# A fused long-convolution and gated-MLP gradient kernel: the order of VectorE's steps in each convolution group, from the product with xn on

## The chip, the cores and the metric

The kernel runs on one core of a Trainium2 chip. The metric is the device time of one execution in microseconds (us), as the median of several. The core has five engines with an instruction stream each: TensorE (PE in the profile, with its weight loads as PEld), VectorE (DVE), ScalarE (ACT), GpSimd (POOL) and SyncE (SP, which here only issues DMA transfers). Matmul results land in PSUM, of which the kernel uses eight banks of 128 x 512 f32; everything else that the engines touch lies in SBUF, and large arrays lie in HBM.

## The reference

The program takes the forward inputs and the gradient of the output, and returns the output and nine gradients, all in bfloat16. S = 2048 rows, D = 1024 channels, F = 3584:

```
x  = A_q
xn = layernorm(x)                                   # over the channels
k_shift[t] = sum_i  k[t - 3 + i] * taps[i]          # 4 taps per channel ("shift")
kv = k_shift * A_v
y  = irfft(rfft(kv, 4096) * rfft(ssm_k, 4096))[:2048] + kv * ssm_D
h  = relu(xn @ W_gate) * (xn @ W_up)
out = x + xn * y + h @ W_down
grads = vjp(out)(grad_out)     # for q, k, v, shift_k, ssm_k, ssm_D, W_gate, W_up, W_down
```

So there are two parts that only share xn. The convolution branch works per channel along time: for the backward pass it needs the gradient of y, which is `grad_out * xn` (the product with xn), its transform, products of spectra for the gradients of kv and of the filter, and then the taps' gradients. The MLP is a chain of large matmuls.

## The kernel before, in words

**MLP.** Class LnMlp. TensorE is fed by it in phases: `hidden` (per 128 rows and 512 of F: gate, up and the gradient of h, eight matmuls of 128x512 each, tiles ps_g, ps_u, ps_h, line L1038), `grad_down` (gradient of W_down, tile ps_d), `grad_in` (gradients of W_gate and W_up, tile ps_w; both L1373, 16 matmuls to a bank), `out_phase` (h @ W_down, tile ps_o, L1537) and `grad_x` (ps_x, L1669). At the ends of `grad_down` and at the start of `grad_in`, where four PSUM banks are accumulated side by side (`four`, L1381 to L1418, matmuls at L1389), the branch may use only two banks at a time instead of three (`self.branch.cap = 2`). In `hidden` VectorE masks up by gate (L1153, tile ru<-ru,ps_u), multiplies (L1159, ht) and, when ScalarE has copied ps_h to gh (L1281), multiplies ru by gh (L1282); the result is stored to ug_d by SP. At the start of `grad_down` grad_out's rows are loaded anew (g_nat, issued by SP at L1068).

**Convolution branch.** Class ABranch. The channels are worked in eight groups of 128, one after the other. The Fourier transforms are small matmuls (all by `mm`, L83) with tables R, FW, IA and RB; ScalarE evicts their results from PSUM (`act`, L87), and VectorE does the products of spectra and the taps (`tt`, L91) and transposes (`flip`, L334: two instructions of 128x1024 f32 for one flip). One large SBUF tile, `arena`, holds all spectra, so most of the branch's rows in the profile read `arena<-arena`.

The blocks on TensorE of one group, in order: `f2` (eight units, three banks' worth at a time; 48, 48 and 32 matmuls with FW), `inv_a` of the gradient, joined with the next group's filter transform (IA and hn,R), `inv_b` for gkv (16 matmuls with RB), `inv[1]` (32 with IA), `cross[0]` and `cross[1]` (half an inverse each, joined with the next group's transform of the product with xn, tile gt), `inv[2]` (32 IA), two `f2` units of the next filter `f2H` (64 FW), again `cross[0]`, `cross[1]` (joined with the next group's kv, tile kp), and then two blocks of 32 FW and 16 RB: `inv_b` for yt (the convolution's output, which goes to y_d) and `inv_b` for gh (the filter's gradient, stored to gh_d).

**How the two are woven.** `slots` (L677) is a generator: each `yield p, d` is one slot, with p the branch's TensorE work (or None) and d its VectorE work: a generator of which one step is taken, a function to be called, or None. `steps` (L577) runs the slots of one group after the other and gives back a nominal time, 1900 ns in `hidden`; in the later phases (`dense`) 1900 for a slot with TensorE work and 1250 for one without. The main loop (after L1764) takes that against what the MLP's generators yield (mostly 1730 ns for eight matmuls): whenever the MLP has caught up, one more slot is emitted. While the branch runs, `pri.strict` pins every instruction, so each engine works in the order in which the program emits it, the MLP's and the branch's together. A VectorE or SP instruction that must wait holds up all that is behind it on its engine. `need` and `fetch` place the loads of the next groups on SP in the same order; a `store` is also emitted at its place.

The VectorE work that the slots name:

- `gate_grad(nx)`: grad_out times xn of the next group, in place, tile gt. With it the part that is changed begins.
- `q`: `cmul`, a product of two half spectra in five steps; here the last, `cmul(H, K, ..., 1)`.
- `tk`: `taps` forward for the next group: four products and three sums, one to a step, seven steps; then `start_kvt`, the product with v.
- `tg`: `taps` backward (tile gk<-gks and gk<-gk,tap), seven steps of 128x2048 bf16.
- `fly`, `flh`, `flG`, `flK`: flips, two steps each; fly is wanted by the yt block, flh by the gh block, flG and flK by the next group's `f2`.

**At the branch's end** `a.close()` frees its SBUF, and `open_right` (L1492) opens the pools of `hT` and `wd` there: W_down is loaded in four pieces of 28 x 128 rows in all (L1498, issued by SP), and `out_phase` loads h transposed (L1503). `out_phase` begins with the first matmul of wd and hT.

Of the kernel before, what the change touches and what calls it, by code (L numbers as in the profile page):

```python
# [48 lines left out]
class ABranch:  # L49
# [627 lines left out]
    def slots(self, st, gi):  # L677
        G, K, H, GKV = self.G, self.K, self.H, self.GKV
        if gi == 0:
            yield from self.first(st)  # L680
        nx, n2 = self.ahead(st, 1), self.ahead(st, 2)
        last = nx is None
        f2 = [(1, self.f2_pair(j, m)) for j in range(4) for m in range(2)]
        if self.cap == 3:
            yield f2[0:3], None
            yield None, None
            yield None, None
            yield f2[3:6], None
        else:
            for i in (0, 2):  # L690
                yield f2[i:i + 2], None
                yield None, None
            yield f2[4:6], None
        yield None, None
        yield None, lambda: self.turn(G, 0, -1, slice(0, 4))
        q = self.cmul(H, G, True, GKV, 0)
        yield f2[6:8], q
        yield None, q
        yield None, q
        yield None, q  # L700
        yield None, q
        yield None, lambda: self.turn(G, 0, -1, slice(4, 8))
        iaG = self.inv_a()
        q = self.cmul(H, G, True, GKV, 1)
        yield None, q
        if last:
            iaG = [iaG[1][0], None, iaG[1][1]]
        else:
            self.need(self.load_filter, nx)
            self.need(self.load_rest, nx)  # L710
            iaG = self.crossed(iaG[0], self.fwd1_filter(nx)[0], 0) + iaG[1][1:]
        yield iaG[0], q
        yield None, q
        yield None, q
        yield iaG[1], q
        yield None, lambda: self.turn(H, 1, 1)
        self.fetch(nx, self.load_k, self.load_taps)
        q = self.cmul(K, G, True, G, 0)
        yield None, q
        yield iaG[2], q  # L720
        yield None, q
        flg = self.flip_C(self.Cg, 0)
        yield None, flg
        yield None, flg
        if not last:
            self.need(self.load_g, nx)
            flH = self.flip_H()
            yield None, self.both(lambda: self.add_D(nx), flH)
            yield None, flH
        yield None, q  # L730
        yield None, q
        q = self.cmul(H, K, False, K, 0)
        yield self.inv_b(st, "gkv", 0), q
        yield None, q
        yield None, q
        gkv = st["gkv"]
        gks = st["gks"] = self.ttile("gks")
        yield None, lambda: self.tt(gks[:, 0:16, :], gkv[:, 0:16, :], st["vt"][:], ALU.mult)
        self.fetch(nx, self.load_v)
        gv = self.ttile("gv")  # L740
        yield None, lambda: self.tt(gv[:, 0:16, :], gkv[:, 0:16, :], st["ksh"][:], ALU.mult)
        yield None, q
        self.store(self.gks_d[gi], gks[:, 0:16, :].rearrange("p r c -> p (r c)"))
        yield None, q
        self.store_time(self.out_gv, st["cg"], gv)
        yield [], lambda: self.halo(st)
        ia, inv = self.inv_a_pair()
        q = self.cmul(K, G, True, G, 1)
        yield inv[1], q
        for _ in range(4):  # L750
            yield None, q
        q = self.cmul(H, K, False, K, 1)
        cross, gk = [inv[0], None], None
        if not last:
            self.need(self.load_xn, nx)
            yield None, lambda: self.gate_grad(nx)
            self.fetch(n2, self.load_xn)
            cross = self.crossed(ia, self.fwd1(self.Bg, nx["gt"])[0], 0)
        yield None, q
        yield None, None  # L760
        yield cross[0], q
        yield None, q
        yield None, q
        yield cross[1], None
        self.fetch(n2, self.load_g)
        yield None, q
        if last:
            f2H, cross = [], [inv[3], None]
            yield inv[2], None
        else:  # L770
            f2H = [(1, self.f2(H, 1, j)) for j in range(4)]
            self.need(self.load_k, nx)
            self.need(self.load_taps, nx)
            self.begin(nx)
            tk = nx["tk"]
            yield None, tk
            yield inv[2], tk
            yield None, tk
            yield None, tk
            yield f2H[0:2], tk  # L780
            yield None, tk
            yield None, tk
            self.need(self.load_v, nx)
            yield None, lambda: self.start_kvt(nx)
            cross = self.crossed(ia, self.fwd1(self.Bk, nx["kvt"])[0], 3)
            yield None, None
        gk = self.ttile("gk")
        tg = self.taps(st, gk, gks, [(0, 0), (1, 1), (2, 2), (3, 3)])
        yield cross[0], tg
        yield None, tg  # L790
        yield None, None
        yield cross[1], tg
        self.fetch(n2, self.load_filter)
        yield None, tg
        yield None, tg
        fly = self.flip_C(self.Cy, 0)
        yield None, fly
        yield None, fly
        yield None, tg
        yield f2H[2:3] + self.inv_b(st, "yt", 0), None  # L800
        self.store_time(self.y_d, st["cg"], st["yt"])
        flh = self.flip_C(self.Ch, 0)
        yield None, flh
        yield None, flh
        yield None, tg
        self.store_time(self.out_gk, st["cg"], gk)
        yield f2H[3:4] + self.inv_b(st, "gh", 0), None
        if last:
            yield None, None
            yield None, lambda: self.store_gh(st)  # L810
            return
        flG = self.flip_B(self.Bg, 0)
        yield None, flG
        yield None, self.both(lambda: self.store_gh(st), flG)
        flK = self.flip_B(self.Bk, 1)
        yield None, flK
        yield None, flK
        yield None, None

A_START = 60_000  # L820
# [996 lines left out]
```

## Time and profile before

| what | value |
|---|---|
| median of 3 runs | 1864.61 us (1864.56 to 1864.93) |
| the profiled execution | 1865.49 us |
| its span, first to last instruction | 1863.7 us |
| TensorE's granted clock | 1.00 |
| busy: PE, DVE, ACT, POOL | 1836.8, 1112.2, 646.7, 19.3 us |

| stretch (us) | phase | PE busy | DVE busy | ACT busy | DMA share |
|---|---|---|---|---|---|
| 60 to 635 | hidden | 567.42 of 575 | 444.22 | 276.93 | 0.78 |
| 635 to 855 | grad_down | 215.12 of 220 | 161.19 | 105.83 | 0.66 |
| 855 to 1280 | grad_in | 419.94 of 425 | 243.72 | 189.66 | 0.59 |
| 1280 to 1467 | out_phase | 186.10 of 187 | 41.15 | 0.59 | 1.10 |
| 1467 to 1863 | grad_x | 391.58 of 396 | 184.25 | 41.96 | 0.74 |

Times in the lines below are us from the span's start, unless a column says otherwise. In a timeline line the first number is the start, the second the duration, then engine, line of the code, operation, tiles (out<-in), shapes and how many instructions the line holds; in square brackets stands how long the engine had been idle before it and who ended that. A line of waits reads: engine, tile and line that waited, who was waited for, then the total in us, how often, and the longest. In a line of windows: stretch, its length, then busy time and count for PE, PEld, DVE, ACT and POOL, the granted clock, the DMA share and GB/s. "xN" in a timeline line is a run of N like instructions. A few matmul records are missing from the trace; such a hole is about 0.22 us wide, one matmul.

### The profile page before, as it was taken

What the parts mean: (1) busy time and instruction counts of PE and PEld (TensorE: products, weight loads), DVE (VectorE), ACT (ScalarE), POOL (GpSimd) and SP (SyncE); (2) the same over time, 40 slices, a digit from 0 to 9 for tenths busy, and PEclk for the clock granted to TensorE, in tenths of its full rate; (3) what the DMA queues carried; (4) which work ended last, traced back from release to release, by engine and by line L of the source; (5) the groups of instructions that cost most, each with busy time, mean ns of one, the idle gap of its engine ahead of it and who ended that gap; (6) DMA issues with size and microseconds to landing.
All of it is one profiled execution on the core that took longest, in us unless ns stands there. A gap on an engine that the chain in (4) does not pass through costs nothing.

```text
span 1863.7 us, 31858 instructions
## 1 busy us (share of the span) xinstructions
PE 1836.8 (99%) x12842; PEld 846.2 (45%) x13061; DVE 1112.2 (60%) x1635; ACT 646.7 (35%) x1215; POOL 19.3 (1%) x51
## 2 busy tenths in 40 slices
PE   9999999999999999999999999999999999999999
PEld 4444444444444444444444444444444544444444
DVE  6656887797788767585594866810212222466652
ACT  5644444535444454545545455320000000111100
POOL 1000000000000000000000000000000000000000
PEclk9999999999999999999999999999999999999999
DMA  9897679968758657558656544479999857799973
GB/s 259 251 220 187 150 200 205 223 163 190 180 150 221 217 147 184 128 163 210 181 146 164 125 133 128 136 176 284 264 240 243 194 135 168 180 209 203 202 163 74
DMA packets 748132, 344.65 MB, mean 185 GB/s; under 512 B 576088, under 2 KB 715344, under 8 KB 747984
## 3 DMA queue, kind: packets, MB, share of 16 engines
q1 hardware_dynamic: 736848, 320.31, 71.4%
q10 hardware_dynamic: 9504, 17.04, 2.9%
q0 software_dynamic: 1632, 5.24, 0.8%
q8 instruction: 102, 1.67, 0.4%
q14 instruction: 46, 0.38, 0.1%
HBM read 143.79 MB, written 103.83 MB: 133 GB/s over the span
## 4 chain that ended last, share of the span: by engine, by line
PE 72%; issue 1%; DVE 0%; DMA 0%; ACT 0%
PE ps_x L1669 21%; PE ps_w L1373 20%; PE ps_o L1537 10%; PE ps_d L1373 9%; PE ps_c L83 3%; PE ps_u L1038 3%; PE ps_h L1038 3%; PE ps_g L1038 2%; PE ps_d L1389 1%; PE ps_w L1389 1%; DVE arena L334 0%; PE ps_r L1571 0%; DMA g_nat<-in_grad_out_dram 0%; ACT arena L87 0%; ACT wi L1413 0%
## 5 line engine op out<-in xcount | busy, mean ns | idle before, releaser
L1373 PE MATMUL ps_w<-ugs,xn_nat 128*128 128x512 bf16 x1674 | 375.8, 379 | 4.4 <-issue 2.4
L87 ACT CAST arena<-ps_c 128x512 bf16<-128x512 f32 x576 | 293.9, 610 | 103.5 <-PE ps_c L83 103.3
L1038 PEld LDWEIGHTS <-xnT 128*128 128x128 bf16 x1792 | 171.4, 98 | 209.4 <-issue 6.4
L334 DVE STREAM_TRANSPOSE arena<-arena 128x1024 f32<-128x1024 f32 x96 | 179.6, 1930 | 134.7 <-ACT arena L87 114.2
L1373 PEld LDWEIGHTS <-xn_nat 128*128 128x128 bf16 x1728 | 165.1, 98 | 201.6 <-issue 7.3
L1038 PE MATMUL ps_u<-wu,xnT 128*128 128x512 bf16 x879 | 205.4, 379 | 0.9
L1038 PE MATMUL ps_g<-wg,xnT 128*128 128x512 bf16 x865 | 202.5, 379 | 1.9 <-DVE xnT L1082 0.3
L1038 PE MATMUL ps_h<-wdT,goT 128*128 128x512 bf16 x864 | 202.3, 379 | 1.8
L1669 PE MATMUL ps_x<-wuT,guT 128*128 128x512 bf16 x878 | 197.5, 379 | 1.0
L1669 PE MATMUL ps_x<-wgT,ggT 128*128 128x512 bf16 x878 | 197.3, 379 | 0.9
L1687 ACT ACTIVATE w<-xn,m 128x512 f32<-128x512 bf16 x32 | 24.3, 807 | 479.5 <-DVE m L1680 366.1
L1537 PE MATMUL ps_o<-wd,hT 128*128 128x512 bf16 (+1 forms) x879 | 186.7, 372 | 0.9
L1373 PE MATMUL ps_d<-g_nat,hs 128*128 128x512 bf16 x742 | 167.2, 379 | 2.2 <-issue 1.3
L1669 PEld LDWEIGHTS <-guT 128*128 128x128 bf16 x896 | 87.7, 98 | 105.7
L1669 PEld LDWEIGHTS <-ggT 128*128 128x128 bf16 x896 | 87.7, 98 | 105.5
L1038 PEld LDWEIGHTS <-goT 128*128 128x128 bf16 x896 | 86.4, 98 | 104.0 <-issue 1.4
L1537 PEld LDWEIGHTS <-hT 128*128 128x128 bf16 x896 | 87.7, 98 | 99.9
L1376 ACT CAST wi<-ps_w 128x512 bf16<-128x512 f32 x108 | 64.4, 596 | 192.3 <-PE ps_w L1373 168.8
L1281 ACT CAST gh<-ps_h 128x512 bf16<-128x512 f32 x112 | 65.9, 591 | 178.7 <-PE ps_h L1038 158.1
L1153 DVE SCALAR_TENSOR_TENSOR ru<-ru,ps_u 128x512 bf16<-128x512 bf16 x112 | 76.4, 682 | 85.5 <-PE ps_u L1038 44.1
L1529 DVE TENSOR_TENSOR ya<-ya,xe 128x1024 bf16<-128x1024 bf16 x16 | 11.1, 692 | 182.6 <-DMA xe<-xn_d 182.6
L91 DVE TENSOR_TENSOR t<-arena 128x2048 bf16<-128x2048 bf16 x96 | 113.9, 1218 | 0.4
(145 smaller groups left out, 1392.1 us busy)
## 6 DMA issues: line engine op xcount, KB each, us to landing
ugs<-ug_d SPq DMA_DIRECT2D x112, 256.0 KB, 4.8
ug_d<-ru SPq DMA_DIRECT2D x110, 256.0 KB, 3.8
wg<-in_B_W_gate_dram SPq DMA_DIRECT2D x56, 256.0 KB, 4.3
wu<-in_B_W_up_dram SPq DMA_DIRECT2D x56, 256.0 KB, 3.3
hs<-h_d SPq DMA_DIRECT2D x56, 256.0 KB, 4.9
out_dram<-wi SPq DMA_DIRECT2D x56, 256.0 KB, 5.2
h_d<-ht SPq DMA_DIRECT2D x108, 128.0 KB, 2.7
gt<-in_grad_out_dram SPq DMA_DIRECT2D x32, 256.0 KB, 6.2
```

Source lines behind the costliest of these rows:

```text
L83: self.pri.pin(self.nc.tensor.matmul(out, lhsT=lhsT, rhs=rhs, start=start, stop=stop))
L87: self.pri.pin(self.nc.scalar.copy(out=out, in_=in_))
L91: self.pri.pin(self.nc.vector.tensor_tensor(out=out, in0=in0, in1=in1, op=op))
L334: self.pri.pin(self.nc.vector.transpose(out=df[:, c0:c0 + 32, :], in_=sf[:, c0:c0 + 32, :]))
L1038: self.pri.pin(self.nc.tensor.matmul(ps[:], lhsT=xT[:, kt * P:(kt + 1) * P], rhs=w(kt), start=(kt == 0), stop=(kt == self.DT - 1)), always ...
L1153: return self.pri.pin(nc.vector.scalar_tensor_tensor(out=ru[s][:, 1, :], in0=ru[s][:, 0, :], scalar=0.0, in1=ps[:], op0=ALU.is_gt, op1=ALU ...
L1281: self.pri.pin(nc.scalar.copy(out=gh[:], in_=ps[:]))
L1373: self.pri.pin(self.nc.tensor.matmul(ps[:], lhsT=lhsT(st), rhs=rhs(st), start=(st == 0), stop=(st == self.ST - 1)))
L1376: self.pri.pin(self.nc.scalar.copy(out=out, in_=ps[:]))
L1389: self.pri.pin(self.nc.tensor.matmul(ps[i][:], lhsT=lhsT(i, st), rhs=rhs(i, st), start=(st == 0), stop=(st == self.ST - 1)))
L1537: nc.tensor.matmul(ps, lhsT=hT[:, kt, :], rhs=self.wd[:, kt, oc], start=(kt == 0), stop=(kt == self.FT - 1))
L1669: nc.tensor.matmul(ps, lhsT=T[:, kt, :], rhs=W[:, kt, oc], start=(i == 0), stop=(i == n - 1))
```

## The change

Only `slots` is changed, in the part from `gate_grad(nx)` on. No VectorE or TensorE instruction is added or removed; what moves is the order of the steps and the slots without VectorE work. By slot, counted from the `gate_grad` slot as 1 (a name is one step of that generator; blocks of TensorE in brackets):

| | before | after |
|---|---|---|
| 1 to 6 | gate_grad; q; none; q [cross 0]; q; q | gate_grad; q; q; q [cross 0]; q; q |
| 7 to 13 | none [cross 1]; q; tk; tk [inv 2]; tk; tk; tk [f2H 0, 1] | tk [cross 1]; tk; tk; tk [inv 2]; tk; tk; tk [f2H 0, 1] |
| 14 to 17 | tk; tk; kvt; none | kvt; none; tg [cross' 0]; none |
| 18 to 24 | tg [cross' 0]; tg; none; tg [cross' 1]; tg; tg; fly | none; tg [cross' 1]; tg; none; fly; fly; tg |
| 25 to 31 | fly; tg; none [yt]; flh; flh; tg; gh block | tg; none [yt]; flh; flh; tg; tg; gh block |
| 32 to 37 | flG; flG; flK; flK; none | flG; flG; flK; flK; none; none |

In the last group, which has no successor, there is one more empty slot before `inv[2]`, and the group ends after the gh block.

```diff
         yield None, q
-        yield None, None
+        yield None, q
         yield cross[0], q
         yield None, q
         yield None, q
-        yield cross[1], None
-        self.fetch(n2, self.load_g)
-        yield None, q
+        f1g, cross = cross[1], [inv[3], None]
+        f2H = []
         if last:
-            f2H, cross = [], [inv[3], None]
+            yield None, None
             yield inv[2], None
         else:
             f2H = [(1, self.f2(H, 1, j)) for j in range(4)]
...
             tk = nx["tk"]
+            yield f1g, tk
+            self.fetch(n2, self.load_g)
+            yield None, tk
             yield None, tk
             yield inv[2], tk
             yield None, tk
             yield None, tk
             yield f2H[0:2], tk
-            yield None, tk
-            yield None, tk
             self.need(self.load_v, nx)
             yield None, lambda: self.start_kvt(nx)
...
         yield cross[0], tg
-        yield None, tg
+        yield None, None
         yield None, None
         yield cross[1], tg
         self.fetch(n2, self.load_filter)
         yield None, tg
-        yield None, tg
+        yield None, None
         fly = self.flip_C(self.Cy, 0)
         yield None, fly
         yield None, fly
+        yield None, tg
         yield None, tg
         yield f2H[2:3] + self.inv_b(st, "yt", 0), None
         self.store_time(self.y_d, st["cg"], st["yt"])
         flh = self.flip_C(self.Ch, 0)
         yield None, flh
         yield None, flh
+        yield None, tg
         yield None, tg
         self.store_time(self.out_gk, st["cg"], gk)
         yield f2H[3:4] + self.inv_b(st, "gh", 0), None
...
         yield None, flK
         yield None, flK
+        yield None, None
         yield None, None
```

## The prediction

> **What bounds the kernel now.** I read the page's busy times and chain first.
>
> ```profile
> PE 1836.8 (99%) x12842; PEld 846.2 (45%) x13061; DVE 1112.2 (60%) x1635; ACT 646.7 (35%) x1215; POOL 19.3 (1%) x51
> PE 72%; issue 1%; DVE 0%; DMA 0%; ACT 0%
> ```
>
> TensorE is busy 99% and the chain lies on it: VectorE's order can move the time only through the few places where TensorE waits. The waits of PE by line come next.
>
> ```profile
> PE ps_c L83 <- DVE arena L334: 3.1, 4, 1.2
> PE ps_d L1389 <- DMA g_nat<-in_grad_out_dram: 1.0, 3, 0.4
> PE ps_c L83 <- ACT arena L87: 0.8, 2, 0.6
> PE ps_c L83 <- DVE arena L91: 0.7, 2, 0.5
> ```
>
> L83 is the branch's matmul, L334 its transpose (flip), L91 its tensor ops. So 5.6 us are at stake, plus what is lost inside blocks, and what the change may add. The PE and VectorE timelines give the places:
>
> ```profile
> 325.39 0.62 PE L83 MATMUL ps_c<-arena,RB 64*32 64x512 bf16 x14 [0.66 <-DVE arena L334]
> 337.63 0.85 PE L83 MATMUL ps_c<-arena,FW 64*32 64x256 bf16 x48 [0.99 <-DVE arena L334]
> 483.49 0.62 PE L83 MATMUL ps_c<-arena,RB 64*32 64x512 bf16 x14 [1.24 <-DVE arena L334]
> ...
> 321.65 3.68 DVE L334 STREAM_TRANSPOSE arena<-arena 128x1024 f32<-128x1024 f32 x2
> 325.19 1.20 DVE L91 TENSOR_TENSOR gk<-gk,tap 128x2048 bf16<-128x2048 bf16 x1
> ...
> 478.56 0.69 DVE L1282 TENSOR_TENSOR ru<-ru,gh 128x1024 bf16<-128x1024 bf16 x1 [2.10 <-ACT gh L1281]
> 479.17 1.94 DVE L334 STREAM_TRANSPOSE arena<-arena 128x1024 f32<-128x1024 f32 x1
> 481.55 1.89 DVE L334 STREAM_TRANSPOSE arena<-arena 128x1024 f32<-128x1024 f32 x1
> ```
>
> RB blocks finish yt or gh, an FW block of 48 opens the next group (f2). The reader sees TensorE reach a block and wait until a transpose ends. At 478.56 VectorE had idled 2.10 us for the MLP's gh with both transposes queued behind it: a matter of order, not of load.
>
> **The change, part by part.** No instruction is added or removed; each group has 37 slots for 36. A slot is one VectorE step, and 8 MLP matmuls pass in it at 0.216 us (10.74 us over 49 in the chain), 1.73 us; sometimes 16 in the hidden phase.
>
> *flh ahead of tg, one more slot to gh.* In the gh block at 324.28 the next MLP matmul came after 1.83 us, in an undisturbed one (888.63) after 0.78: 1.05 lost; likewise 2.41 at 481.80: 1.63 lost. The tap product that ran before the transposes (1.2 us) goes behind, yt's step is one slot earlier and gh's slot number stays, so flh has 1.2 to 1.2 + 1.73 us more: the first stall goes whole, the second gives between 1.2 and 1.63; I take 1.5, since the transposes also move ahead of that 2.10 us wait. Gain 1.05 + 1.5 = 2.55.
>
> *One more slot ahead of f2.* The 0.99 us at 337.63 meets 1.73 more: gain 1.0. Two small ones at 656.07 (0.22) and 896.69 (0.27) go as well: 0.5.
>
> *The four-bank matmuls (`four`).* gh is split there by its two-bank cap, and its second half waits 0.20 for ACT; from 644.72 its eight matmuls take 0.82 where sixteen take 0.61 undisturbed: 0.5 lost; its halves now lie 9 MLP matmuls apart instead of 2 (my count in program order): gain 0.5 (bounds 0 to 0.85). At 845.90 a crossed block takes 2.15 us to the next MLP matmul where one at 873.26 takes 0.57; less a matmul that the records lack (0.22) it loses 1.35 to evictions by ACT: another crossed block falls into that place, so nothing is gained (bounds 0 to 1.35). The kvt block at 866.90 (1.30, reckoned likewise) loses 0.5 and leaves `four`'s end: gain 0.5 (0 to 0.7).
>
> *g_nat.* The 1.0 us are loads of grad_out, queued on SP behind the ug_d store, which waits for an L1282 product that VectorE does after two transposes. In the new order it is done before them, so the loads go up to 1.0 us sooner: gain 0.6 (0 to 1.0).
>
> *q, tk and kvt one or two slots earlier, tg spread over idle slots.* q, tk and kvt run against operands done slots before; kvt to its cross block keeps one idle slot and at least 1 us in the hidden groups. tg has slack: only gk's store waits for it. I take 0 (bound: a 1.2 us product late once in each of the 3 hidden groups, 3.6).
>
> *Lag by one slot a group.* The group's first half now meets other MLP work. Its critical place is inv[1], where TensorE waits for the last cmul. In group 1 these rows stand close:
>
> ```profile
> 408.95 1.28 DVE L91 TENSOR_TENSOR arena<-t 128x1024 bf16<-128x1024 bf16 x2
> ...
> 410.44 0.64 PE L83 MATMUL ps_c<-arena,IA 32*64 32x256 bf16 x32
> ```
>
> Done at 410.23, used at 410.44. From the last point where VectorE waited for TensorE (385.77) it has one transpose more to do (1.8, from its start to the next instruction's, the 3.68 for two less the last one's overlap) and one L1282 product (0.6): 412.6, while TensorE arrives 8 matmuls later, 412.17: a new stall of 0.45. Group 2 (ready 568.74, used 569.18, two slots of lag, 3.45) gets a cmul sum pair 1.33, a transpose 1.8, an eviction pair 1.05 and two products 1.2 more, starting 0.7 sooner: 573.4 against 572.63: 0.8. Loss 1.25 (bounds 0 to 3: one transpose late in both groups, less the slack).
>
> *The tail.* The branch's last block moves from MLP matmul 5189 to 5237 (program order), 48 x 0.2157 = 10.4 us later; its end opens the hT and wd pools, and wd feeds out_phase. SP's own queue:
>
> ```profile
> 1223.22 5.86 SPq L1503 DMA_TRANSPOSE hT<-h_d  x1
> 1229.75 8.74 SPq L1503 DMA_TRANSPOSE hT<-h_d  x2
> 1240.69 6.31 SPq L1355 DMA_DIRECT2D ugs<-ug_d  x8
> 1249.70 0.36 SPq L107 DMA_DIRECT2D gh_d<-gh  x1
> 1255.67 8.35 SPq L1498 DMA_DIRECT2D wd<-in_B_W_down_dram  x4
> ...
> 1280.02 7.29 PE L1537 MATMUL ps_o<-wd,hT 128*128 128x512 bf16 x33
> ```
>
> wd (7.3 MB) is issued from 1255.67, when gh_d has landed, and is in at about 1276.8 (packet records); TensorE wants its first quarter at 1280.02, its last at 1284.5. In the new program order the eight ugs loads (6.3 us) and the y_d stores come ahead of the hT transposes instead of behind. So hT starts at 1233.5, gh_d is issued about 1251.5 and lands about 1258.5, wd goes from there, held once or twice by an out_dram store: last quarter at 1279 to 1281, about 3.5 us early. I take 0; bounds: 0, and with gh_d's end taken 10.4 us later in full 1276.8 + 10.4 - 1284.5 = 2.7 us, or at a slower rate of the load (below) about 9.
>
> Sum: 2.55 + 1.0 + 0.5 + 0.5 + 0.5 + 0.6 - 1.25 = 4.4 us gained. The profiled execution took 1865.49 (span 1863.7 and 1.8 around it), 0.88 above the median 1864.61. 1865.49 - 4.4 = 1861.1, as a median 1860.2.
>
> The granted clock (last figure but two) is full in windows that hold waits of 1.24 us:
>
> ```profile
> 470.00:500.00 30.00, 28.49 (x260) 13.10 (x264) 24.29 (x25) 13.77 (x27) 0.00 (x0) 1.00 0.76 194
> 1250.00:1300.00 50.00, 49.79 (x229) 22.70 (x232) 2.77 (x4) 5.28 (x9) 0.00 (x0) 1.00 0.91 278
> ```
>
> (The figure after the clock is the DMA share.)
>
> [...]
>
> **Rivals.** *Same:* VectorE is loaded in the hidden phase (444 of 575 us), so stalls only change place: inv[1] takes 3 us instead of 1.25 and the `four` places stay (their 1.0): 4.4 - 1.75 - 1.0 = 1.6 gained, 1863.0. For it: the 0.2 and 0.45 us of slack. Against it: the end stalls come of order, not of load. *Slower:* wd late. Before, it took 21.1 us from issue to landing. The gain of 4.4 is eaten when its last quarter lands at 1284.5 + 4.4 = 1288.9, and the kernel is slower by 0.2% past 1284.5 + 8.1 = 1292.6, that is when the load from 1258.5 takes over 34 us; at 0.6 of its rate it takes 35.2, 9.2 us are lost and the time is 1864.6 - 4.4 + 9.2 = 1869.4. For it: DMA is 91% busy in the window below, and the load now meets other stores and stands nearer to its use. Against it: ugs is out of the way, and the trace had 3 to 7 us to spare. *No effect:* VectorE keeps its pinned order of MLP work, so the same losses return elsewhere: 1864.6. For it: the number of instructions is the same. Against it: at 478.56 the order itself costs.
>
> **How the numbers follow.** 0.2% (3.73 us) is about what a measurement tells from no change: faster is below 1860.88, slower above 1868.34. My forecast of 1860.2 is only 0.7 inside. Forecast case 0.56, stalls change place 0.15, no effect 0.09, wd late 0.20. Of the first 0.50 counts as faster and 0.06 as same, where a term or two falls to its lower end; of wd late 0.18 is slower by more than 0.2%: faster 0.50, same 0.32, slower 0.18. Range: low 1857.0, every stall gone and inv[1] without loss (5.6 + 2 = 7.6 gained); high 1868.4, which takes in the second and third case and leaves out the 0.18.
>
> **What would show it.** Right: no L334 wait before gh and f2 at about 324, 338 and 482; new L91 waits of 0.4 to 1 us at inv[1] near 411 and 570; SP's wd from about 1258, ps_o starting without a DMA wait. Wrong: an L1537 wait on wd, or L83 waits on L91 or L334 in more than two places of a hidden group.

## The result, and the profile after

| kernel | median (us) | lowest to highest | runs |
|---|---|---|---|
| before | 1864.71 | 1864.20 to 1864.93 | 6 |
| changed | 1872.70 | 1871.31 to 1874.49 | 6 |

The ratio of changed to before is 1.0044, with a 95% interval of 1.0031 to 1.0057: slower by 8.0 us where 4.4 us of gain were forecast. The profiled execution of the changed kernel took 1871.87 us, 0.8 below its median; its span is 1869.7, 6.0 more than before. Line numbers behind L820 are 3 higher than before; the runs' kernels below differ in the same way, by up to 10 lines.

The place is found from the starts of the phases (the first matmul of each, before and after): ps_d 637.00 and 641.28, ps_w 855.63 and 860.67, ps_o 1280.02 and 1286.03, ps_x 1467.43 and 1473.44. So 4.3 us are lost in the hidden phase, 0.8 in grad_down, 1.0 in grad_in, nothing behind. The waits of PE in the changed kernel:

```profile
PE ps_g L1041 <- ACT ru L1149: 4.9, 1, 4.9
PE ps_d L1392 <- DMA g_nat<-in_grad_out_dram: 1.8, 4, 0.8
PE pst_x L1080 <- DVE ln_x L940: 1.8, 1, 1.8
...
PE ps_c L83 <- DVE arena L91: 1.2, 4, 0.4
PE ps_w L1392 <- DMA xn_nat<-xn_d: 0.7, 2, 0.4
```

The row "ps_c <- DVE arena L334", 3.1 us before, is gone: what the change was expected to remove there, it removed. A row that was not there before holds more than that in one piece: TensorE waits 4.9 us once, for a bank that a relu (L1149) has to empty. (The wait of pst_x is the first layernorm's, at 7 us; before it was 1.1.) The page's first line does not help here:

```profile
PE 1853.3 (99%) x13061; PEld 846.7 (45%) x13061; DVE 1113.7 (60%) x1635; ACT 646.3 (35%) x1215; POOL 19.4 (1%) x51
```

Busy time of PE rose by 16.5 us, but before 12842 matmul records were kept and here 13061; holes of one matmul lie in one trace and not in the other. The waits and the starts of phases are to be compared, not this sum.

**The 4.9 us.** PE's and ACT's timelines of the changed kernel there:

```profile
345.20 0.85 PE L83 MATMUL ps_c<-arena,FW 64*32 64x256 bf16 x48
345.98 1.90 PE L1041 MATMUL ps_u<-wu,xnT 128*128 128x512 bf16 x8
352.80 5.08 PE L1041 MATMUL ps_g<-wg,xnT 128*128 128x512 bf16 x16 [4.92 <-ACT ru L1149]
...
343.58 0.60 ACT L1149 ACTIVATE ru<-ps_g 128x512 bf16<-128x512 f32 x1 [0.33 <-PE ps_g L1041]
352.15 0.60 ACT L1149 ACTIVATE ru<-ps_g 128x512 bf16<-128x512 f32 x1 [7.97 <-DMA ug_d<-ru]
352.64 3.03 ACT L87 CAST arena<-ps_c 128x512 bf16<-128x512 f32 x6
```

and ACT's before:

```profile
345.53 0.60 ACT L1146 ACTIVATE ru<-ps_g 128x512 bf16<-128x512 f32 x1 [1.14 <-PE ps_g L1038]
346.02 3.03 ACT L87 CAST arena<-ps_c 128x512 bf16<-128x512 f32 x6
352.59 0.60 ACT L1146 ACTIVATE ru<-ps_g 128x512 bf16<-128x512 f32 x1 [3.54 <-DMA ug_d<-ru]
```

The relu at about 352 waits in both kernels, at the same time, for the same thing: a store of ug_d that must free an ru tile. SP issues that store at 348.68 before and at 348.61 after; its queue shows no idle stretch of more than 0.4 us from 327 to 357. Before, the six evictions of group 1's second f2 block run ahead of that relu. After, the block comes one slot later, its six evictions stand behind the relu in ScalarE's pinned order, its six banks stay taken, and TensorE, with two banks left, stops.

**The clock.** Windows of the changed kernel over the gap and behind it (the granted clock stands last but two):

```profile
345.00:351.00 6.00, 2.88 (x58) 1.39 (x57) 1.11 (x2) 0.00 (x0) 0.00 (x0) 1.00 0.90 254
351.00:353.00 2.00, 0.20 (x1) 0.10 (x1) 0.00 (x0) 0.85 (x2) 0.00 (x0) 0.85 1.08 248
353.00:355.00 2.00, 2.00 (x6) 0.72 (x5) 1.22 (x3) 2.00 (x5) 0.00 (x0) 0.50 0.97 315
355.00:357.00 2.00, 2.00 (x9) 0.81 (x8) 0.76 (x1) 1.27 (x3) 0.00 (x0) 0.80 0.90 198
```

In the last two rows the clock is 0.5 and on average 0.8, over 2 us each: an estimated 2 x 0.5 + 2 x 0.2 = 1.4 us lost on top of the wait. The matmuls agree: the sixteen from 352.80 took 5.08 us, the sixteen from 341.65 at full clock 3.62.

**The second place,** where g_nat is loaded, in PE's timeline, SP's queue and two windows of the changed kernel:

```profile
650.22 0.38 PE L1392 MATMUL ps_d<-g_nat,hs 128*128 128x512 bf16 x1 [0.77 <-DMA g_nat<-in_grad_out_dram]
650.90 0.81 PE L1392 MATMUL ps_d<-g_nat,hs 128*128 128x512 bf16 x3 [0.30 <-DMA g_nat<-in_grad_out_dram]
651.87 0.38 PE L1392 MATMUL ps_d<-g_nat,hs 128*128 128x512 bf16 x1 [0.16 <-DMA g_nat<-in_grad_out_dram]
652.85 0.59 PE L1392 MATMUL ps_d<-g_nat,hs 128*128 128x512 bf16 x1 [0.60 <-DMA g_nat<-in_grad_out_dram]
...
642.82 1.34 SPq L107 DMA_DIRECT2D y_d<-yt  x2
644.25 1.35 SPq L1290 DMA_DIRECT2D ug_d<-ru  x1
645.65 2.96 SPq L1071 DMA_DIRECT2D g_nat<-in_grad_out_dram  x4
...
649.00:652.50 3.50, 2.01 (x8) 0.58 (x6) 0.94 (x1) 1.84 (x4) 0.00 (x0) 1.00 0.99 330
652.50:656.00 3.50, 3.15 (x14) 0.86 (x14) 1.95 (x2) 1.66 (x3) 0.00 (x0) 0.54 1.07 356
```

The wait is 1.8 us for 1.0 before, and the clock falls here too, to 0.54 over 3.5 us: an estimated 1.6 us more, of which the 24 matmuls from 653.93 show 1.1 (6.44 us, for 5.34 of the 24 from 365.29 at full clock). Before, the second half of the gh block (eight RB matmuls) still stood ahead of the wait, and the like window held 2.48 us of busy PE and kept its clock, 1.00 (PE's timeline, SP's queue and the window):

```profile
644.72 0.89 PE L83 MATMUL ps_c<-arena,RB 64*32 64x512 bf16 x8 [0.20 <-ACT arena L87]
...
647.05 0.81 PE L1389 MATMUL ps_d<-g_nat,hs 128*128 128x512 bf16 x3 [0.40 <-DMA g_nat<-in_grad_out_dram]
...
636.81 1.34 SPq L107 DMA_DIRECT2D y_d<-yt  x2
638.24 3.81 SPq L1287 DMA_DIRECT2D ug_d<-ru  x2
642.10 2.05 SPq L1068 DMA_DIRECT2D g_nat<-in_grad_out_dram  x4
...
645.50:649.00 3.50, 2.48 (x16) 0.88 (x10) 3.34 (x2) 1.61 (x4) 0.00 (x0) 1.00 0.99 322
```

The forecast waits at inv[1] in groups 1 and 2 are there, 0.38 and 0.50 us by the blocks' lengths (from the block's first matmul to the next MLP one 0.95 and 1.07 us, where the same blocks took 0.57 before):

```profile
417.25 0.53 PE L83 MATMUL ps_c<-arena,IA 32*64 32x256 bf16 x24 [0.17 <-DVE arena L91]
577.03 0.53 PE L83 MATMUL ps_c<-arena,IA 32*64 32x256 bf16 x24 [0.29 <-DVE arena L91]
```

### The profile page after: what moved, and what is told of

It reads as the page before. It is cut to its first block, busy times and chain, and to the rows that moved or that the text cites. A ratio compares the mean times of both kernels' runs of the same rounds, so it can differ in the third digit from the quotient of the medians.

```text
span 1869.7 us, 32060 instructions
## 1 busy us (share of the span) xinstructions
PE 1853.3 (99%) x13061; PEld 846.7 (45%) x13061; DVE 1113.7 (60%) x1635; ACT 646.3 (35%) x1215; POOL 19.4 (1%) x51
## 4 chain that ended last, share of the span: by engine, by line
PE 95%; DVE 2%; DMA 2%; ACT 1%; issue 0%; SPq 0%; ACTq 0%; DVEq 0%
PE ps_x L1672 21%; PE ps_w L1376 20%; PE ps_o L1540 10%; PE ps_g L1041 10%; PE ps_u L1041 10%; PE ps_h L1041 9%; PE ps_d L1376 9%; PE ps_c L83 4%; PE ps_d L1392 1%; DVE ru L1156 0%; DMA g_nat<-in_grad_out_dram 0%; DVE arena L334 0%; PE ps_r L1574 0%; PE ps_w L1392 0%; DMA xn_nat<-xn_d 0%
## 5 line engine op out<-in xcount | busy, mean ns | idle before, releaser
L1376 PE MATMUL ps_w<-ugs,xn_nat 128*128 128x512 bf16 x1728 | 381.3, 379 | 0.0
L334 DVE STREAM_TRANSPOSE arena<-arena 128x1024 f32<-128x1024 f32 x96 | 179.5, 1931 | 137.0 <-ACT arena L87 118.0
L1041 PE MATMUL ps_g<-wg,xnT 128*128 128x512 bf16 x896 | 206.5, 381 | 5.6 <-ACT ru L1149 4.9
L1156 DVE SCALAR_TENSOR_TENSOR ru<-ru,ps_u 128x512 bf16<-128x512 bf16 x112 | 76.5, 683 | 81.6 <-PE ps_u L1041 56.0
```

The source lines that it names most:

```text
L334: self.pri.pin(self.nc.vector.transpose(out=df[:, c0:c0 + 32, :], in_=sf[:, c0:c0 + 32, :]))
L1041: self.pri.pin(self.nc.tensor.matmul(ps[:], lhsT=xT[:, kt * P:(kt + 1) * P], rhs=w(kt), start=(kt == 0), stop=(kt == self.DT - 1)), always ...
L1156: return self.pri.pin(nc.vector.scalar_tensor_tensor(out=ru[s][:, 1, :], in0=ru[s][:, 0, :], scalar=0.0, in1=ps[:], op0=ALU.is_gt, op1=ALU ...
L1376: self.pri.pin(self.nc.tensor.matmul(ps[:], lhsT=lhsT(st), rhs=rhs(st), start=(st == 0), stop=(st == self.ST - 1)))
```

## The experiments

The medians, all against a kernel before at 1864.6 to 1864.8 in the same sets of runs:

| run | edit | median (us) | ratio to before, 95% interval |
|---|---|---|---|
| e1 | changed, without the 37th slot | 1861.86 | 0.9984, 0.9975 to 0.9992 |
| e2 | before, with the 37th slot only | 1871.81 | 1.0036, 1.0024 to 1.0049 |
| e3 | changed, group 1's second f2 block one slot earlier | 1866.91 | 1.0011, 1.0002 to 1.0020 |
| e4 | changed, group 2's filter loads later | 1867.59 | 1.0013, 1.0004 to 1.0022 |
| e5 | before, flh ahead of a tap step | 1865.68 | 1.0005, 0.9996 to 1.0014 |
| e6 | e1, the two first f2 blocks closer | 1861.78 | 0.9984, 0.9975 to 0.9992 |
| e7 | e6, inv[1] one slot later | 1860.55 | 0.9975, 0.9965 to 0.9985 |
| e8 | e3, group 2's y_d stores later | 1862.14 | 0.9984, 0.9975 to 0.9993 |

### Without the 37th slot, and with nothing else

```diff
         yield None, flK
         yield None, flK
         yield None, None
-        yield None, None
```

> The changed kernel without its 37th slot (the second empty slot at the end of a group). Theory E (the second f2 block now lies behind a relu on ScalarE that waits for a store of ug_d; its six banks stay taken and TensorE stops for 4.9 us, and the clock falls after it): the block is one slot earlier again, ahead of that relu, so no wait of ps_g for ru, and a full clock there; the f2 wait of about 1 us comes back, the gh waits stay away: about 1862.5. Theory S (the store is simply late on SP's queue, because TensorE now comes 2 us sooner; where f2 lies does not matter): the wait of ps_g for ru stays, 3 us or more, about 1868.

Measured 1861.86. The waits of PE have no row for ru and none for g_nat, and the clock is 1.00 in every window; f2's wait is back, and one for goT is new:

```profile
PE ps_c L83 <- DVE arena L334: 1.2, 2, 1.0
...
PE ps_h L1040 <- DMA goT<-in_grad_out_dram: 0.8, 1, 0.8
```

That is as theory E has it; theory S expected the wait for ru to stay. So the changed order without the slot is 2.8 us faster than before, and the one empty slot costs 10.8 us. The opposite run puts the slot into the kernel before:

> The kernel before with nothing but the second empty slot at the end of a group. Theory E: the wait of ps_g for ru appears, about 3.9 us (TensorE comes a stall of 1.05 us later than in the changed kernel), with a low clock after it; the waits before gh (1.05 and 1.6) stay, those before f2 (1.5 in all) go, inv[1] waits about 0.9: about 1869.5. Theory S: TensorE is hardly sooner than before, so the wait is at most 1 us and the time about 1864.

Measured 1871.81, with this row of waits and this window behind it:

```profile
PE ps_g L1039 <- ACT ru L1147: 4.7, 1, 4.7
...
351.00:357.00 6.00, 3.49 (x9) 1.29 (x9) 1.99 (x3) 3.52 (x7) 0.00 (x0) 0.61 0.96 265
```

Theory S expected 1864 and fell: the wait does not need the time that the new order saved. Theory E named the wait, and undersized it by 0.8 us. In the old order the slot costs 7.2 us (1871.81 less 1864.63), not 10.8: this run has no wait for g_nat; its y_d stores go out at 653.37, behind the loads of g_nat (645.48), an order that the last run on g_nat below (e8) tests by itself. The longer wait at the second place needs the slot and the new order together.

### The place of one f2 block, and the store itself

```diff
             yield f2[0:3], None
             yield None, None
-            yield None, None
-            yield f2[3:6], None
+            if gi == 1:
+                yield f2[3:6], None
+                yield None, None
+            else:
+                yield None, None
+                yield f2[3:6], None
```

> The changed kernel with the second f2 block of group 1 alone one slot earlier (one empty slot is taken from before it and put behind it). Theory E: the evictions of f2 run ahead of the waiting relu, the wait of ps_g for ru is gone or below 1 us, the clock stays at 1.00 near 350: 6.3 us less than the changed kernel, about 1866.4. Theory S: the relu waits for the same store, ps_g for the relu: 4 to 5 us of wait stay, about 1872.

Measured 1866.91. ACT's timeline of this run shows the store as late as ever, and the evictions out of its way:

```profile
343.93 3.03 ACT L87 CAST arena<-ps_c 128x512 bf16<-128x512 f32 x6
352.19 0.60 ACT L1153 ACTIVATE ru<-ps_g 128x512 bf16<-128x512 f32 x1 [5.23 <-DMA ug_d<-ru]
...
PE ps_d L1396 <- DMA g_nat<-in_grad_out_dram: 2.5, 3, 1.8
...
PE ps_u L1045 <- ACT ru L1153: 1.1, 1, 1.1
```

The relu still waits until 352.2, TensorE waits 1.1 us instead of 4.9, and the clock stays at 1.00 there. That is 5.8 us for the place of one block: theory E is shown. The last two rows are the waits of PE; g_nat's has grown to 2.5 us.

In the next run the loads of group 2's filter, hn, leave the queue ahead of the store: their `fetch` goes, for group 0, from behind the second cross' block to the end of the group's slots.

> The changed kernel with the loads of the filter of group 2 (four on SP, some 4.2 us of its queue near 337 to 343) issued at the end of group 0's slots, behind the ug_d store that the relu waits for. Theories E and S both expect the store up to 4 us sooner, the wait of ps_g for ru 1 us or less and the clock at 1.00 near 350: about 1866.5. If the wait stays above 3 us, the store is not held by SP's queue.

Measured 1867.59. SP's queue and ACT's timeline of this run:

```profile
342.18 0.75 SPq L1293 DMA_DIRECT2D ug_d<-ru  x1
...
344.46 0.57 SPq L1293 DMA_DIRECT2D ug_d<-ru  x1
345.13 6.20 SPq L99 DMA_DIRECT2D hn<-in_A_ssm_k_dram  x4
...
345.46 0.60 ACT L1152 ACTIVATE ru<-ps_g 128x512 bf16<-128x512 f32 x1 [1.42 <-DMA ug_d<-ru]
```

The store is issued 6.4 us sooner, the relu runs at 345.5, and ru costs TensorE 0.4 us. Both links of the chain are so shown apart: the store is late by SP's order, and the evictions behind the relu turn that into a stop. This run waits 3.2 us for g_nat.

### The loads of g_nat

```diff
-        self.store_time(self.y_d, st["cg"], st["yt"])
+        if gi != 2:
+            self.store_time(self.y_d, st["cg"], st["yt"])
...
         yield None, self.both(lambda: self.store_gh(st), flG)
+        if gi == 2:
+            self.store_time(self.y_d, st["cg"], st["yt"])
```

> The changed order with the second f2 block of group 1 one slot earlier (1866.9; it waits 2.5 us for g_nat near 645, and the clock is 0.5 for 3.4 us behind it), and the two y_d stores of group 2 issued on SP some five slots later, so that they no longer stand ahead of the ug_d store and the g_nat loads. Theory N (the loads are held by SP's order, because the lag puts the yt block and its stores nearer to them): g_nat is issued 0.9 us or more sooner, the wait falls to 1.5 us or less; 1865.9 with the clock still low, 1864.2 if it stays full. If the loads land no sooner, DMA bandwidth holds them and the time is 1866.9.

Measured 1862.14, 4.8 us below e3 and more than expected. SP's queue of this run, and a window with it:

```profile
634.39 2.22 SPq L1297 DMA_DIRECT2D ug_d<-ru  x2
636.67 2.82 SPq L1078 DMA_DIRECT2D g_nat<-in_grad_out_dram  x4
...
640.00:647.50 7.50, 7.34 (x78) 3.23 (x78) 6.27 (x5) 3.55 (x7) 0.00 (x0) 1.00 1.05 344
```

The loads are issued 0.5 us after the first matmul of ps_d (636.15) where e3 had 4.4 (640.11 after 635.74). In e3 the y_d stores go out at 637.27, behind the eviction of yt that they wait for (in the changed kernel it ends at 642.79 and they go out at 642.82), and on SP they held the ug_d store and the loads behind them. With them out of the way no wait for g_nat is left, and the clock stays at 1.00. In e3 it had fallen after the wait:

```profile
643.50:647.50 4.00, 1.82 (x7) 0.58 (x6) 0.90 (x1) 1.80 (x4) 0.00 (x0) 1.00 0.96 299
647.50:651.50 4.00, 3.73 (x17) 1.16 (x17) 2.53 (x2) 1.66 (x3) 0.00 (x0) 0.57 1.09 358
```

2.5 us of wait and an estimated 4 x 0.43 = 1.7 us of clock make 4.2 of the 4.8. Not every execution of e3 pays the second term: the two of its eleven whose mean clock is 1.000 took 1864.0 and 1864.3 us.

### What the new order gains, and a faster kernel

The next run asks whether the order behind the cross blocks alone brings e1's gain. It is an edit of the kernel before:

```diff
-        yield None, tg
         yield f2H[2:3] + self.inv_b(st, "yt", 0), None
         self.store_time(self.y_d, st["cg"], st["yt"])
         flh = self.flip_C(self.Ch, 0)
         yield None, flh
         yield None, flh
         yield None, tg
+        yield None, tg
```

> The kernel before with one edit: the sixth tap step of the backward taps goes from ahead of the yt block to behind flh, so yt and flh come one slot sooner; 36 slots, q, tk and kvt as before. Theory G (the gain of the changed order is the two gh waits alone): the waits of 1.05 us (group 0) and 1.63 us (group 1) before gh go, f2's 1.0 us stays: 1862.0, the same as the changed order without its 37th slot (1861.9). Rival: the earlier q, tk and kvt carry part of that gain: 1863.5 or more.

Measured 1865.68: theory G fell. PE's and VectorE's timelines of this run, and two windows:

```profile
315.75 0.62 PE L83 MATMUL ps_c<-arena,RB 64*32 64x512 bf16 x14 [2.27 <-DVE arena L334]
...
313.80 1.89 DVE L334 STREAM_TRANSPOSE arena<-arena 128x1024 f32<-128x1024 f32 x1
...
313.00:316.00 3.00, 0.73 (x27) 0.29 (x33) 2.97 (x4) 0.00 (x0) 0.00 (x0) 1.00 0.24 66
316.00:319.00 3.00, 2.71 (x44) 1.21 (x30) 0.64 (x2) 2.33 (x5) 0.00 (x0) 0.59 0.88 255
```

The yt block, one slot sooner, now waits for fly as gh had waited for flh, and the clock falls after 2.27 us in this execution (four of the eleven have a mean clock below 1.000; the median has not). The gh waits are gone, as forecast; the wait has changed its place. In e1, where the cross' blocks and fly come two slots sooner as well, neither wait is there. That fits the rival, but no run shows the earlier steps without the new tail, so which of them is needed stays open.

Two more runs look for what is left in e1. In the hidden phase the first f2 block comes one slot later and the second stays:

```diff
+            yield None, None
             yield f2[0:3], None
             yield None, None
-            yield None, None
             yield f2[3:6], None
```

> The changed order with 36 slots (no lag), and in the hidden phase the first f2 block one slot later, the second where it is with 36 slots. The 1.0 us wait before f2 should go without the lag: evictions of the second block stay ahead of the relu that waits for ug_d: 1861.9 - 1.0 = 1860.9, ps_g or ps_u wait for ru 1.1 us at most. If 7 matmuls between two blocks of six banks are too few, or the relu is reached sooner, TensorE waits 3 us or more for ru and the time is about 1866.

Measured 1861.78, as e1 and 0.9 above what was expected. The waits of 1.0 for f2 and of 0.8 for goT are gone; waits of 0.8 (ps_g for VectorE's copy of the transposed xn) and 0.7 (ps_u for ru) stand in their place. With inv[1] one slot later on top of that:

```diff
-        yield inv[1], q
-        for _ in range(4):
+        yield None, q
+        yield inv[1], q
+        for _ in range(3):
             yield None, q
```

> As the run with the two f2 blocks close together, and inv[1] one slot later in each group. The wait for the last cmul in group 0 (1.0 us near 250) should go and nothing else appear: 1859.9. If inv[1]'s result is needed by something at once, a new wait of about a slot (1.7 us) shows.

Measured 1860.55, 1.2 us less than e6, 0.6 above what was expected. The block of group 0 that lost 1.0 us at 250.66 before runs without a wait:

```profile
252.43 0.64 PE L83 MATMUL ps_c<-arena,IA 32*64 32x256 bf16 x32
```

The wait of 0.8 for xn is gone too, and one of 0.4 for wu (a load of W_up) is new, so the 1.2 us are not that block's alone. This kernel is faster than both, by 4.2 us against before.

## Why the prediction was wrong

**The step that failed is "Lag by one slot a group".** It said that the lag's critical place is inv[1] and priced it there at 1.25 us; inv[1] cost 0.38 + 0.50 = 0.9, close to that. But a lag moves every block of the group past the MLP's instructions on every engine, and I followed it on VectorE alone. On ScalarE it put six evictions behind a relu that waits for a store: 4.9 us of wait and 1.4 of clock. On SP, in the new order, it left the y_d stores, which wait for yt, close ahead of the g_nat loads, and on TensorE it moved the half of gh that had given these loads time behind the wait for them. The runs give the price in whole kernels: 10.8 us for the 37th slot (changed less e1; 7.2 in the old order), of which 5.8 are the place of one f2 block (changed less e3) and 4.8 the order around g_nat (e3 less e8). The waiting relu stood in the trace of before, with 3.54 us of idle ScalarE and DMA ug_d<-ru as the releaser. It cost nothing there, so no row of PE's waits named it, and I read no other engine's waits.

**"flh ahead of tg, one more slot to gh"** (2.55): the waits at 324 and 482 are gone as forecast. The reason was half of it: e5 shows that this order alone moves the wait to yt. In e1 and the changed kernel, with the earlier steps and the cross' blocks two slots sooner, the yt block does not wait; the prediction priced those steps at 0 and did not look at yt's wait for fly.

**"One more slot ahead of f2"** (1.5): those waits are gone, and this slot is the one that costs 10.8 us. The 0.22 at 656.07 was no wait: the block starts 1.82 us after the eight matmuls ahead of it (654.25), as it does undisturbed (337.31 to 339.13 in the changed kernel); of those eight one record is missing.

**The length of a slot**: 10.74 us over 49 matmuls is 0.219 us each; the 0.216 that the prediction used is the distance of the starts (50 in the 10.79 us from 1225.63 to 1236.42, one of them without a record). No term changes by it.

**"The four-bank matmuls"**: the kvt block lost its 0.5 us (875.48 to the next MLP matmul at 876.05: 0.57), a crossed block still loses 1.35, and gh's second half takes 0.56 us (653.37 to 653.93) for 0.82. All as forecast in the changed kernel.

**"g_nat"** (a gain of 0.6): the sign was wrong. The loads are issued 4.4 us after the first ps_d matmul instead of 5.1, so 0.7 us sooner, but not for the reason given. Stores of ug_d follow the L1282 products one by one (112 of each), so the last one ahead of the loads before, at 640.21, belongs to the product that VectorE had done at 637.99, ahead of both transposes. What held the loads were the y_d stores, issued at 636.81 when yt was evicted, and the 1.9 us that each of two ug_d stores then took on SP; after, one of the two goes out ahead of y_d. And TensorE now asks for the row 8.2 us after that matmul (650.22 - 0.77 - 641.28) instead of 9.7 (647.05 - 0.40 - 637.00), mostly since the gh half that stood in between (1.0 us with its wait) moved behind: 0.8 us more of wait, and 1.6 of clock. Two terms that I had added were one: what TensorE saved ahead of the transfer, it waited for at the transfer.

**"The tail"** (0): right. The last quarter of wd is issued at 1273.45, ps_o starts at 1286.03 right behind ps_w, and no wait names wd; the slower rival that I had priced was not the one that came:

```profile
1273.45 1.08 SPq L1501 DMA_DIRECT2D wd<-in_B_W_down_dram  x1
```

**The clock** was left out of the sum. It fell twice in the profiled execution, an estimated 1.4 + 1.6 = 3.0 us; the two slowest executions of the changed kernel (1874.4 and 1874.5 us) have a mean clock of 0.997 and 0.996 where this one has 0.998. In the profiled execution the named terms of the hidden phase make 4.9 + 1.4 + 0.9 lost less 1.05 + 1.06 + 1.63 gained (1.06 for f2, by its start 2.88 and 1.82 us after that of the eight matmuls ahead of it), 3.5 of the 4.3 measured; 0.3 more lies in a later start of the first ps_g (8.11 for 7.85), 0.2 in a new wait of ps_g for ru (L1156), and 0.3 is not assigned. In grad_in, of the 1.0 us, one more branch block lies in that phase (0.57, at 865.30) and two waits of 0.7 in all for xn_nat are new, against 0.5 and 0.27 gained; 0.5 is not assigned.

## What to carry to other kernels

Before a block is moved by one place, list what its evictions will stand behind on the engine that empties the banks: an instruction there that waited for a transfer cost nothing before (3.54 us of idle ScalarE, and no row of PE's waits) while nothing needed was queued behind it, and 4.9 us of TensorE once something was. So read the waits of every pinned engine and queue, also where TensorE does not wait. And do not add the gain of removed waits to the gain at a transfer that follows them: time saved ahead of the late load came back here as a longer wait for it (1.8 us for 1.0). An idle slot "for slack" is a shift of everything behind it, and is tried first without the shift, as e6 and e7 do.

## What was not expected of the hardware

The granted clock fell to 0.5, a term that the prediction's sum does not have. In the changed kernel it was 0.50 from 352.40 to 355.80, behind 4.92 us of idle TensorE, and 0.50 from 652.80 to 656.10, behind four waits of 0.77, 0.30, 0.16 and 0.60 us, in 3.5 us of which PE's rows hold 2.01 us of work. In other profiled executions it was low behind a single wait of 2.27 us (e5: 0.59 from 316 to 319, 0.84 from 319 to 322), behind one of 4.71 us (e2: 0.61 from 351 to 357, 0.73 from 357 to 361) and behind the waits for g_nat (e3: 1.82 us of work in 4 us, then 0.57 from 647.5 to 651.5; e4: 0.86 from 635 to 660). It was 1.00 with 2.48 us of work in 3.5 us (before, the g_nat waits), with 1.55 us of work in 3 us (the changed kernel's start, from 6 to 9) and around a single wait of 1.24 us (before, from 470 to 500). In the changed kernel and e3 each fall cost an estimated 1.4 to 1.7 us, by the windows; in e2 an estimated 2.8 us behind the wait, if the clock was 0.5 without a break from about 352.3 to 359.2, which agrees with its two windows.

What decides whether the clock falls is not shown. The share of work does not order these windows by itself: 0.46 in e3 and 0.57 in the changed kernel with a fall, 0.52 at the changed kernel's start without one. Nor does every execution of a kernel have a fall: of the eleven executions each of e5, e3 and e4, four, nine and eight have a mean clock below 1.000, but all five of e2 and all six of the changed kernel.
